# Element-wise work dealt out again between VectorE and GpSimd beside a matmul stream (attention and a split-precision FFN, one core)

## The chip, the cores and the metric

The kernel runs on one core of a Trainium2 chip. The engines are named as the profile names them: PE (TensorE's matmuls; its weight loads are PEld), DVE (VectorE), ACT (ScalarE), POOL (GpSimd) and SP (SyncE, which only issues DMAs here). The metric is the device time of one execution in microseconds (us). The kernel before took 859.63, 861.60 and 862.29 us in three runs, median 861.60.

## The reference

Local attention over 8 batches of 8 heads with 576 positions of 64 features, then a two-layer feed-forward network with an ELU on the 4608 resulting tokens, all in float32:

```python
rel = pos[:, None] - pos[None, :]
mask_plain = (rel >= 0) & (rel < 32)                     # heads 0 to 3
mask_dil = (rel >= 0) & (rel < 128) & (rel % 4 == 0)     # heads 4 to 7
scores = where(masks, q @ k.T / 8, -1e9)
attn = exp(scores - max(scores)); attn = attn / (sum(attn) + 1e-09)
x = (attn @ v) laid out as 4608 tokens x 512
h = x @ w_in                                             # 512 -> 2048
g = where(h > 0, h, exp(minimum(h, 0)) - 1)
out = g @ w_out                                          # 2048 -> 512
```

## The kernel before, in words

**Precision.** A float32 product is made of three matmuls on operands split in two: ACT casts a tile to a rounded high part (CAST in the profile), DVE subtracts it from the tile (the "rest", a TENSOR_TENSOR with an fp32r output), and PE adds high x high, high x low and low x high. A tile can be used by PE once its cast and its rest are done, in that order.

**The token axis** is cut in nine chunks of 512. Chunks 0, 1 and 2 go through the network plainly (`plain_chunk`: 16 steps f of 12 matmuls into one bank `h`, an ELU, and 12 matmuls into the output banks `o_ps`). The other six chunks are three "wide blocks" w = 0, 1, 2 of two chunks each (`wide_chunk`). There a two-by-two block product is done with seven block products in place of eight (A11, A12, S2, S1, S3, A22, S4 of the weights, against B11, B21, T2, T1, T3, T4, B22 of the tokens; S and T are sums and differences of blocks). A step of a block product is 12 matmuls of 128x128 by 128x512. "Inner" steps are the first layer, "outer" steps the second one; a block has 28 of each, and the list `wide` sets their order. An inner step's banks are added up, copied and put through the ELU by `behind_inner`, into four blocks (B11, B12, B21, B22) per group g = 0..3, tiles `a`, `a-1`, `r` of 128x1024.

**The units of the second layer.** The 28 outer steps take 28 right-hand units k in the order A11 and A12 (k = 0..7), S1 (8..11), S2 (12..15), A22 (16..19), S3 (20..23), S4 (24..27). `make_unit` makes one: `summed(k + 1)` first issues the subtraction of the next unit if it is one of the 16 of S1, S2, A22 and S3 (two blocks of 128x1024, in place), then ACT casts unit k and DVE makes its rest. A block subtracts on POOL in w = 0 and on DVE in w = 1 and 2. Units are made up to LEAD = 4 outer steps ahead in w = 0 and up to 7 in the others.

**The weight sums** S1 to S4 are made on the chip too, in jobs of "sums" steps on POOL from chunk 1 up to the first half of block 0: quarter weights loaded from memory (`whole`, `whole_out`), added, cast, their rests taken, written back (`sums_out`).

**Attention** is 32 pairs of heads and batches, laid between the network's steps. For a pair PE makes the scores (24 matmuls into two `a_ps` banks), DVE adds the masks, and `pair_steps` follows: max, less, exp, sum, more, over, times (on a tile of 96x768), six "placed" copies of 32x384 into `pt`, and "turned" (a transpose). PE then multiplies `pt` by the values `vt` (24 matmuls), and ACT copies the result to `x32`, the tokens. `pieces` lets in one set of scores or outputs at given places of PE's stream, if `scores_ready` or `output_ready` says so.

**What sets the order.** All of it is written out at build time, engine by engine, by a planner that keeps a modelled `clock` for each engine. The class `Ordered` (line 590) wraps an engine: each instruction goes through its `emit` (line 606 in the profile, whatever it does; matmuls are line 146) and moves the clock on by a fixed cost and one per element. `work(until)` (line 640) takes the step that can start first. `better` (line 632) lets POOL have a step of the kinds in SHARED (placed copies, less, times, late) as long as the phase is below SHARED_UNTIL: phase 2 is chunk two, 3 is wide block 0, 3.2 and 3.4 its later parts, 4 and 5 blocks 1 and 2. SLOWING charges a tenth of POOL's work to DVE's clock, FILL is how far past PE's clock steps are dealt out, TOLERANCE and EARLY how far past it a piece may be ready, in blocks and in chunks. On the chip each engine then runs its own list in that order and waits by semaphores for what it needs: an instruction that waits holds up all behind it on its engine.

The right-hand operands of block 0 are made by `wide_operand` at the end of chunk two and in the first five inner steps (tables at line 70): "make" is the subtraction (T1 to T4, on DVE), "cast" on ACT, "rest" on DVE. T2 and T4 start from T1 and T2.

Of the kernel before, what the change touches and what calls it, by code (L numbers as in the profile page):

```python
# [69 lines left out]
WIDE_FIRST = {"A11": "make:T1 make:T2 cast:T2 rest:T2", "A12": "cast:T1 rest:T1 make:T3", "S2": "cast:T3 rest:T3 make:T4", "S1": "cast:T4 rest:T4", "S3": "cast:B22 rest:B22"}  # L70
STORE_LAG = 1
FILL = 4.2
# [6 lines left out]
TOLERANCE = 0.3  # L79
EARLY = 0.0  # L80
# [3 lines left out]
SLOWING = 0.1  # L84
SHARED, SHARED_UNTIL = ("placed", "less", "times", "late"), 2.5
# [8 lines left out]
def body(ctx: ExitStack, tc: tile.TileContext, q, k, v, masks, w_in, w_out, out, out_t):  # L94
# [446 lines left out]
    def masks_added(hp, places, sm, eng=nc.vector):  # L541

        dil = hp >= NPAIR // 2
        for i in range(max(len(p) for p in places)):
            for h in range(2):
                n0, n1, s_ps = places[h][i]
                last = eng.tensor_tensor(out=sm[:, h * NU + n0:h * NU + n1, :].rearrange("p n j -> p (n j)"), in0=s_ps[:QB, :(n1 - n0) * 2 * G],
                                        in1=mask_sb[:, int(dil), n0 * 2 * G:n1 * 2 * G], op=ALU.add)
# [41 lines left out]
    class Ordered:  # L590
# [7 lines left out]
        def cost(self, kw):  # L598
            return self.fixed + self.each * (kw if isinstance(kw, int) else max(length(kw[n]) for n in ("out", "in_", "in0") if n in kw))

        def __getattr__(self, name):
            def emit(**kw):
                if self.name == "POOL":
                    clock["DVE"] += SLOWING * self.cost(kw)
                clock[self.name] = self.free() + self.cost(kw)
# [3 lines left out]
    vec, act, pool = Ordered(nc.vector, "DVE", 0.155, 0.00104), Ordered(nc.scalar, "ACT", 0.19, 0.00083), Ordered(nc.gpsimd, "POOL", 0.55, 0.0017)  # L609
# [16 lines left out]
    def cost(step):  # L626

        return step[1].cost(step[4] if callable(step[3]) else step[3])
# [98 lines left out]
    def pair_steps(b, hp, sm):  # L727
# [9 lines left out]
        yield ("more", b, hp), vec, "tensor_scalar", dict(out=sums, in0=sums, scalar1=1e-9, scalar2=None, op0=ALU.add)  # L737
# [59 lines left out]
    def scores_ready():  # L797
# [5 lines left out]
        if not rooms:  # L803
# [105 lines left out]
    def store(c, t, o_ps):  # L909
# [3 lines left out]
        later.append((STORE_LAG, lambda: nc.sync.dma_start(out=out[c * TC + t * P:c * TC + (t + 1) * P, :], in_=o)))  # L913
# [68 lines left out]

    def wide_operand(w, what):
# [5 lines left out]
        t = space(name in ("T2", "T4")) if name[0] == "T" else None  # L989
        j, k = {"B11": (0, 0), "B21": (1, 0), "B22": (1, 1)}.get(name, (0, 0))  # L990
        if do == "make":
            for r0, r1, (left, right) in wide_stretches(w, 0, 1):
                x0, x1 = {"T1": lambda: (right(0), left(0)), "T2": lambda: (right(1), space(0)[:, :, r0:r1]), "T3": lambda: (right(1), right(0)),
                          "T4": lambda: (left(1), space(1)[:, :, r0:r1])}[name]()
# [563 lines left out]
```

## Time and profile before

| | us |
|---|---|
| three runs, median | 859.63, 861.60, 862.29; 861.60 |
| profiled execution: its time, its span | 860.48, 858.6 |
| PE busy | 827.7 (96%) |
| DVE busy | 649.5 (76%) |
| ACT busy | 539.9 (63%) |
| POOL busy | 230.9 (27%) |
| mean granted clock | 0.988 |

The profiled execution lies 1.1 us under the median of the runs; its span, from the first to the last instruction, is 1.9 us shorter than its own time. Rows of a timeline read: start us, duration us, engine, line, operation, output <- inputs by the program's tile names, sizes, count, and in brackets the idle time before it with what ended it. Rows of the waits read: engine, what it worked on, what it waited for: total us, times, longest. Rows of windows read: start:end and length, then for each engine its busy time and its count of instructions, the granted clock as a share of full speed, the DMA share and GB/s. Chunk 0 runs up to about 80 us, chunk two ends near 355 us, block 0 near 525 us, block 1 near 690 us.

### The profile page before, as it was taken

The numbers are of one execution on the slowest core, as the hardware profiler recorded it, in microseconds if no ns is written. First come the engines' busy times: TensorE is split into PE (matmuls) and PEld (weight loads), VectorE is DVE, ScalarE is ACT, GpSimd is POOL, SyncE is SP. The second block draws the span as 40 slices with busy tenths as digits, with TensorE's granted clock in tenths as the row PEclk, the third lists the DMA queues.
The fourth block names the chain that finished last, engine by engine and source line by source line (L and its number), as shares of the span: only waits on it lengthen the run. The fifth ranks groups of instructions, "written<-read, shape, count | busy, mean of one in ns | idle before, by whom it ended". The sixth has DMA issues, their size and how long they took to land.

```text
span 858.6 us, 16052 instructions
## 1 busy us (share of the span) xinstructions
PE 827.7 (96%) x6304; PEld 653.9 (76%) x6304; DVE 649.5 (76%) x769; ACT 539.9 (63%) x912; POOL 230.9 (27%) x200
## 2 busy tenths in 40 slices
PE   6999999999999999999989789999999999999998
PEld 5566888777778778777777568878888888888886
DVE  6999996877858579868798887456769864466992
ACT  5888776765566556588777255458954545676450
POOL 3000001346376453655524980210010020000000
PEclk9999999999999999999999879999999999999999
DMA  8999879745367695799958636966656677666665
GB/s 305 372 383 366 263 232 281 213 163 163 127 220 222 170 321 187 253 399 328 293 177 244 219 97 185 327 182 185 194 175 206 205 247 220 192 189 195 200 209 169
DMA packets 105322, 199.14 MB, mean 232 GB/s; under 512 B 13120, under 2 KB 58528, under 8 KB 104992
## 3 DMA queue, kind: packets, MB, share of 16 engines
q1 hardware_dynamic: 105104, 197.81, 72.0%
q8 instruction: 50, 0.82, 0.4%
q10 hardware_dynamic: 144, 0.31, 0.1%
q14 instruction: 24, 0.20, 0.1%
HBM read 148.54 MB, written 49.55 MB: 231 GB/s over the span
## 4 chain that ended last, share of the span: by engine, by line
PE 83%; DVE 8%; ACT 5%; DMA 2%; issue 2%; DVEq 0%; SPq 0%; ACTq 0%
PE o_ps L146 43%; PE h L146 26%; PE a_ps L146 13%; DVE a L606 2%; DVE x L606 2%; DMA outputs<-a-1_3421 2%; ACT x L606 2%; DVE r L606 1%; ACT pt L533 1%; PE b L146 1%; ACT a L606 1%; DVE a-1_3421 L606 0%; DMA qt<-q 0%; DVE sm L606 0%; DVE pt L606 0%
## 5 line engine op out<-in xcount | busy, mean ns | idle before, releaser
L146 PE MATMUL o_ps<-a,r 128*128 128x512 f32 x792 | 191.6, 397 | 4.3 <-DVE a L606 3.3
L146 PEld LDWEIGHTS o_ps<-a,r 128*128 128x128 f32 x792 | 150.6, 191 | 37.6 <-DVE a L606 3.6
L146 PE MATMUL o_ps<-r,r 128*128 128x512 f32 x432 | 106.1, 397 | 4.8 <-DVE r L606 2.5
L146 PEld LDWEIGHTS o_ps<-r,r 128*128 128x128 f32 x432 | 82.2, 191 | 23.7 <-DVE r L606 3.2
L146 PE MATMUL h<-a,r 128*128 128x512 f32 x396 | 94.7, 391 | 1.1 <-ACT r L606 1.1
L146 PEld LDWEIGHTS h<-a,r 128*128 128x128 f32 x396 | 73.8, 188 | 17.3 <-ACT r L606 1.5
L146 PE MATMUL h<-x,r 128*128 128x512 f32 x324 | 80.3, 395 | 0.0
L146 PE MATMUL o_ps<-a,gh 128*128 128x512 f32 x216 | 76.2, 450 | 0.0
L146 PEld LDWEIGHTS h<-x,r 128*128 128x128 f32 x324 | 59.9, 188 | 14.6 <-DVE x L606 1.1
L606 ACT ACTIVATE x<-x 128x1024 f32<-128x1024 f32 (+1 forms) x52 | 54.3, 1046 | 13.4 <-DVE x L606 12.7
L146 PE MATMUL a_ps<-a,r 128*128 128x512 f32 x252 | 60.4, 393 | 1.2 <-DVE a L606 1.2
L606 POOL TENSOR_TENSOR a<-a 128x256 f32<-128x256 f32 (+1 forms) x57 | 52.5, 924 | 31.9 <-DMA a<-whole_out 20.3
L146 PEld LDWEIGHTS a_ps<-a,r 128*128 128x128 f32 x252 | 47.7, 190 | 12.3 <-DVE a L606 2.0
L146 PEld LDWEIGHTS o_ps<-a,gh 128*128 128x128 f32 x216 | 39.6, 188 | 17.9 <-issue 10.5
L606 POOL TENSOR_TENSOR a<-a,a 128x1024 f32<-128x1024 f32 (+2 forms) x6 | 14.9, 2488 | 128.1 <-ACT a L606 120.6
L606 DVE TENSOR_TENSOR a<-r,a 128x1024 fp32r<-128x1024 f32 x30 | 42.3, 1411 | 8.7 <-ACT a L606 8.6
L606 POOL TENSOR_TENSOR x<-x 128x256 f32<-128x256 f32 (+3 forms) x14 | 15.1, 1082 | 112.2 <-DVE a L606 98.5
L146 PE MATMUL o_ps<-r,gh 128*128 128x512 f32 x136 | 42.8, 396 | 0.0
L146 PEld LDWEIGHTS a_ps<-pt,vt 128*64 128x64 f32 x672 | 28.8, 137 | 16.8 <-issue 13.1
L606 ACT CAST a<-r 128x1024 fp32r<-128x1024 f32 x30 | 31.5, 1050 | 14.5 <-DVE r L606 12.3
L606 ACT COPY pt<-sm 32x384 f32<-32x384 f32 x65 | 33.2, 510 | 11.7 <-DVE sm L606 10.6
L146 PE MATMUL a_ps<-pt,vt 128*64 128x96 f32 x672 | 34.4, 250 | 6.3 <-issue 3.1
(229 smaller groups left out, 1647.8 us busy)
## 6 DMA issues: line engine op xcount, KB each, us to landing
r<-combined SPq DMA_DIRECT2D x84, 512.0 KB, 4.3
r<-sums_out SPq DMA_DIRECT2D x48, 512.0 KB, 4.5
r<-plain_out SPq DMA_DIRECT2D x36, 512.0 KB, 3.7
vt<-v SPq DMA_DIRECT2D x30, 384.0 KB, 4.7
kt<-k SPq DMA_DIRECT2D x29, 304.0 KB, 4.4
qt<-q SPq DMA_DIRECT2D x30, 288.0 KB, 4.0
r<-w_in SPq DMA_DIRECT2D x16, 512.0 KB, 7.1
r<-w_out SPq DMA_DIRECT2D x16, 512.0 KB, 7.4
```

The costliest lines, as they stand in the source:

```text
L146: return inorder(nc.tensor.matmul(to, w, x, **kw))
L533: inorder(nc.scalar.copy(out=to[ks, :, :, cs], in_=t4[rs, :, :, cs]))
L606: return inorder(getattr(self.eng, name)(**kw))
```

## The change

VectorE's `tensor_tensor` of the planned part is issued as `scalar_tensor_tensor` (the first input times 1.0, then the operation), except where an input lies in a PSUM bank; those go through the new `from_bank` and stay as they were. The step "more" becomes one as well. `freer` chooses DVE or POOL, whichever the planner's clocks say would end the work first, for the "make" of T1 to T4 and for the subtractions of `summed`, in all three blocks. SHARED_UNTIL goes from 2.5 to 3.5, so that POOL can get attention steps in chunk two's second half and in block 0. POOL's modelled costs change and SLOWING goes. T1 and T2 of block 0 are made in chunk two's steps 14 and 15 (in the space `a4'`), and T3, T4 and B22 each one inner step earlier. Scores are let in only while DVE's clock is at most BACKLOG = 5 us ahead of PE's; FILL, TOLERANCE and EARLY get smaller. The DMA of chunk outputs is issued one slot earlier.

```diff
                "T3": (("a0", 0, 2), ("a1", 0, 2)), "T4": (("a7", 0, 2), ("a6", 0, 2)), "B22": (("r3", 0, 1), ("r3", 2, 3))}
-WIDE_FIRST = {"A11": "make:T1 make:T2 cast:T2 rest:T2", "A12": "cast:T1 rest:T1 make:T3", "S2": "cast:T3 rest:T3 make:T4", "S1": "cast:T4 rest:T4", "S3": "cast:B22 rest:B22"}
+BEFORE = {13: "cast:B11 rest:B11", 14: "cast:B21 rest:B21 make:T1", 15: "make:T2 cast:T2 rest:T2"}
+WIDE_FIRST = {"A11": "cast:T1 rest:T1 make:T3", "A12": "cast:T3 rest:T3 make:T4", "S2": "cast:T4 rest:T4", "S1": "cast:B22 rest:B22"}
 STORE_LAG = 1
-FILL = 4.2
+FILL = 3.5
 WIDE_STEP = 4.0
...
 PIECES = {2 * G: 0.034, QB: 0.12}
-TOLERANCE = 0.3
-EARLY = 0.0
+TOLERANCE = 0.0
+EARLY = -1.0
 HOME = {2: 1, 3: 2, 4: 2.4, 5: 3.2, 6: 3.2, 7: 4.2}
...
 LEAD = 4
-SLOWING = 0.1
-SHARED, SHARED_UNTIL = ("placed", "less", "times", "late"), 2.5
+BACKLOG = 5.0
+SHARED, SHARED_UNTIL = ("placed", "less", "times", "late"), 3.5
 SUMS_FROM = 7
...
                 n0, n1, s_ps = places[h][i]
-                last = eng.tensor_tensor(out=sm[:, h * NU + n0:h * NU + n1, :].rearrange("p n j -> p (n j)"), in0=s_ps[:QB, :(n1 - n0) * 2 * G],
+                add = eng.from_bank if isinstance(eng, Ordered) else eng.tensor_tensor
+                last = add(out=sm[:, h * NU + n0:h * NU + n1, :].rearrange("p n j -> p (n j)"), in0=s_ps[:QB, :(n1 - n0) * 2 * G],
                                         in1=mask_sb[:, int(dil), n0 * 2 * G:n1 * 2 * G], op=ALU.add)
...
-        def cost(self, kw):
+        def cost(self, kw, name=None):
+            if self.name == "POOL" and name in ("copy", "tensor_copy"):
+                return 0.3 + 0.0009 * (kw if isinstance(kw, int) else length(kw["out"]))
             return self.fixed + self.each * (kw if isinstance(kw, int) else max(length(kw[n]) for n in ("out", "in_", "in0") if n in kw))
+        def from_bank(self, **kw):
+            clock[self.name] = self.free() + self.cost(kw)
+            return inorder(self.eng.tensor_tensor(**kw))
...
             def emit(**kw):
-                if self.name == "POOL":
-                    clock["DVE"] += SLOWING * self.cost(kw)
-                clock[self.name] = self.free() + self.cost(kw)
+                if self.name == "DVE" and name == "tensor_tensor":
+                    return self.scalar_tensor_tensor(out=kw["out"], in0=kw["in0"], scalar=1.0, in1=kw["in1"], op0=ALU.mult, op1=kw["op"])
+                clock[self.name] = self.free() + self.cost(kw, name)
                 return inorder(getattr(self.eng, name)(**kw))
...
-    vec, act, pool = Ordered(nc.vector, "DVE", 0.155, 0.00104), Ordered(nc.scalar, "ACT", 0.19, 0.00083), Ordered(nc.gpsimd, "POOL", 0.55, 0.0017)
+    vec, act, pool = Ordered(nc.vector, "DVE", 0.155, 0.00104), Ordered(nc.scalar, "ACT", 0.19, 0.00083), Ordered(nc.gpsimd, "POOL", 0.45, 0.00185)
+    def freer(out):
+        return min((vec, pool), key=lambda eng: eng.free() + eng.cost(length(out)))
...
-        return step[1].cost(step[4] if callable(step[3]) else step[3])
+        return step[1].cost(step[4] if callable(step[3]) else step[3], step[2])
...
         yield ("sum", b, hp), vec, "tensor_reduce", dict(out=sums, in_=sm, op=ALU.add, axis=mybir.AxisListType.X)
-        yield ("more", b, hp), vec, "tensor_scalar", dict(out=sums, in0=sums, scalar1=1e-9, scalar2=None, op0=ALU.add)
+        yield ("more", b, hp), vec, "scalar_tensor_tensor", dict(out=sums, in0=sums, scalar=1e-9, in1=sums, op0=ALU.add, op1=ALU.max)
         yield ("over", b, hp), vec, "reciprocal", dict(out=sums, in_=sums)
...
         rooms = free_sms()
-        if not rooms:
+        if not rooms or vec.free() > clock["PE"] + BACKLOG:
             return False
...
         act.copy(out=o, in_=o_ps)
-        later.append((STORE_LAG, lambda: nc.sync.dma_start(out=out[c * TC + t * P:c * TC + (t + 1) * P, :], in_=o)))
+        later.append((0, lambda: nc.sync.dma_start(out=out[c * TC + t * P:c * TC + (t + 1) * P, :], in_=o)))
...
+    def temporary(w, name):
+        if w == 0 and name in ("T1", "T2"):
+            return slots("a4'", *((0, 1) if name == "T1" else (2, 3)))
+        return space(name in ("T2", "T4"))
...
         h, l = wides[name]
-        t = space(name in ("T2", "T4")) if name[0] == "T" else None
+        t = temporary(w, name) if name[0] == "T" else None
         j, k = {"B11": (0, 0), "B21": (1, 0), "B22": (1, 1)}.get(name, (0, 0))
...
             for r0, r1, (left, right) in wide_stretches(w, 0, 1):
-                x0, x1 = {"T1": lambda: (right(0), left(0)), "T2": lambda: (right(1), space(0)[:, :, r0:r1]), "T3": lambda: (right(1), right(0)),
-                          "T4": lambda: (left(1), space(1)[:, :, r0:r1])}[name]()
-                (vec, pool)[w > 0].tensor_tensor(out=t[:, :, r0:r1], in0=x0, in1=x1, op=ALU.subtract)
+                x0, x1 = {"T1": lambda: (right(0), left(0)), "T2": lambda: (right(1), temporary(w, "T1")[:, :, r0:r1]), "T3": lambda: (right(1), right(0)),
+                          "T4": lambda: (left(1), temporary(w, "T2")[:, :, r0:r1])}[name]()
+                freer(t[:, :, r0:r1]).tensor_tensor(out=t[:, :, r0:r1], in0=x0, in1=x1, op=ALU.subtract)
         elif t is not None:
...
             for i in range(2):
-                vec.tensor_tensor(out=to[i], in0=tos[i], in1=us[key][i], op=ALU.add)
+                vec.from_bank(out=to[i], in0=tos[i], in1=us[key][i], op=ALU.add)
...
                 if to is not None:
-                    (pool if w == 0 else vec).tensor_tensor(out=to, in0=x, in1=y, op=ALU.subtract)
+                    freer(to).tensor_tensor(out=to, in0=x, in1=y, op=ALU.subtract)
...
                     cols = slice(i * TC // n, (i + 1) * TC // n)
-                    vec.tensor_tensor(out=o[:, cols], in0=tos[r][:, cols], in1=us[key][r][:, cols], op=ALU.add)
+                    vec.from_bank(out=o[:, cols], in0=tos[r][:, cols], in1=us[key][r][:, cols], op=ALU.add)
                     def write(o=o, t=t, s=s, cols=cols):
...
             finished[id(side[-1])] = clock["PE"] + LATENCY
-            if c == CS - 1 and f in (13, 14):
-                name = ("B11", "B21")[f - 13]
-                wide_operand(0, "cast:" + name)
-                wide_operand(0, "rest:" + name)
+            if c == CS - 1:
+                for what in BEFORE.get(f, "").split():
+                    wide_operand(0, what)
             pend.append((c, f, None))```

Counted over the lists of instructions: POOL has 205 rows where it had 162. Of the placed copies 39 go from ACT to POOL (POOL 11 to 50, ACT 133 to 94), of the steps less and times POOL has 11 where it had 5. Of the 16 subtractions of `summed`, block 0 keeps 9 on POOL and puts 7 on DVE (units 11, 12, 13, 14, 16, 19 and 22); in blocks 1 and 2, where DVE had all 16, POOL gets 7 of each. One attention pair whose scores lay in the last part of block 0 is let in later, in block 1. Three places follow.

POOL, last part of block 0, before, and then after. `a3`, `r1`, `r2`, `a-1` are the blocks of groups 0 to 3; the rows of 128x1024 are `summed`:

```order
L606 TENSOR_TENSOR a3_4138<-a3_4138 128x1024
L606 TENSOR_TENSOR r1_4364<-r1_4364 128x1024
L606 TENSOR_TENSOR r2_4673<-r2_4673 128x1024
L606 TENSOR_TENSOR a-1_3421<-a-1_3421 128x1024
L606 TENSOR_TENSOR a3_4138<-a4_4139,a3_4138 128x1024
L606 TENSOR_TENSOR r1_4364<-r1_4364 128x1024
L606 TENSOR_TENSOR r2_4673<-r2_4673 128x1024
L606 TENSOR_TENSOR a-1_3421<-a5_2073,a-1_3421 128x1024
```

```order
L614 TENSOR_TENSOR x1_4040<-x1_4040,nmx_4986 96x768
L614 COPY pt0_79<-x1_4040 32x12x32 x3
L614 TENSOR_TENSOR a3_4087<-a3_4087 128x1024
L614 TENSOR_TENSOR r1_4308<-r1_4308 128x1024
L614 TENSOR_TENSOR r2_4589<-r2_4589 128x1024
L614 TENSOR_TENSOR a-1_3413<-a5_2068,a-1_3413 128x1024
L614 COPY pt1_80<-sm_1487 32x12x32
L614 TENSOR_TENSOR r1_4308<-r1_4308 128x1024
```

Before, the subtractions of units 8 to 15 (S1, then S2) stand together on POOL, and those of 16 to 23 follow them. After, POOL keeps units 8, 9, 10 and 15 of these eight, then 17, with attention steps ahead of and between them.

DVE at units 12 to 14, before, and then after. Rows that write `a6` or `r3` from a block (`a3`, `r1`, `r2`) are the rests of units 12, 13 and 14; `nmx`, `sums`, `x1`, `sm` of 96 partitions are attention:

```order
L606 TENSOR_TENSOR a6_1544<-a3_4138,a7_1539 128x2x512
L606 TENSOR_REDUCE nmx_5323<-x1_4089 96x12
L606 TENSOR_TENSOR x1_4089<-x1_4089,nmx_5323 96x768
L606 TENSOR_REDUCE sums_5324<-x1_4089 96x12
L606 TENSOR_SCALAR sums_5324<-sums_5324 96x12
L606 RECIPROCAL sums_5324<-sums_5324 96x12
L606 TENSOR_TENSOR x1_4089<-x1_4089,sums_5324 96x768
L606 TENSOR_TENSOR r3_1352<-r1_4364,r3_1352 128x1024
L606 TENSOR_TENSOR sm_1487<-a_ps0_5381,masks_sb_76 96x384
L606 TENSOR_TENSOR sm_1487<-a_ps1_5382,masks_sb_76 96x384
L606 TENSOR_TENSOR r3_1352<-r2_4673,r3_1352 128x1024
```

```order
L614 SCALAR_TENSOR_TENSOR a6_1544<-a3_4087,a7_1539 128x2x512
L607 TENSOR_TENSOR sm_1487<-a_ps0_5304,masks_sb_76 96x384
L607 TENSOR_TENSOR sm_1487<-a_ps1_5305,masks_sb_76 96x384
L614 SCALAR_TENSOR_TENSOR r2_4589<-r2_4589 128x1024
L614 SCALAR_TENSOR_TENSOR r3_1352<-r1_4308,r3_1352 128x1024
L614 TENSOR_REDUCE nmx_5344<-sm_1487 96x12
L614 SCALAR_TENSOR_TENSOR sm_1487<-sm_1487,nmx_5344 96x768
L614 TENSOR_REDUCE sums_5345<-sm_1487 96x12
L614 SCALAR_TENSOR_TENSOR sums_5345<-sums_5345 96x12
L614 RECIPROCAL sums_5345<-sums_5345 96x12
L614 SCALAR_TENSOR_TENSOR sm_1487<-sm_1487,sums_5345 96x768
L614 SCALAR_TENSOR_TENSOR r3_1352<-r2_4589,r3_1352 128x1024
```

Before, the steps of one pair (from max to times) stand between the rests of units 12 and 13, and those of a second pair (whose masks are the last but one rows here) behind the rest of 14. After, the first pair stands some twenty rows earlier, the subtraction of unit 14 is on DVE, and the second pair's steps stand between the rests of 13 and 14.

POOL around the making of T3 and T4, after (`x0` is T3, `x1` T4, `a4_3926` here T1 and T2; rows of `a5` are sums jobs). Before, POOL had sums jobs alone here, and all of T1 to T4 was on DVE:

```order
L614 TENSOR_TENSOR a5_2068<-a5_2068 128x256
L614 TENSOR_TENSOR x0_4039<-x32_2762 128x2x192
L614 TENSOR_TENSOR x0_4039<-x32_2762 128x2x64
L614 TENSOR_TENSOR sm_1487<-sm_1487,sums_3847 96x768
L614 TENSOR_TENSOR a5_2068<-a5_2068 128x256 x2
L614 TENSOR_TENSOR x1_4040<-x32_1957,a4_3926 128x2x192
L614 CAST gh_4110<-a5_2068 128x512
```

So T3's first two stretches and T4's first one now stand on POOL behind sums steps; the other stretches stay on DVE.

## The prediction

> **What bounds the kernel now.** I read the page's busy shares and its chain first, then the waits of PE, then timelines of the places where PE waits. The page:
>
> ```profile
> PE   6999999999999999999989789999999999999998
> PEclk9999999999999999999999879999999999999999
> PE 83%; DVE 8%; ACT 5%; DMA 2%; issue 2%; DVEq 0%; SPq 0%; ACTq 0%
> ```
>
> PE is on the chain for 83% of the span and full but for one hole near slice 23, where the granted clock falls too. An element-wise change can only win where PE waits, or where PE runs slow after a wait. PE's waits, longest first (those of the first 80 us, which the change does not touch, left out):
>
> ```profile
> PE o_ps L146 <- DVE a L606: 3.3, 1, 3.3
> PE o_ps L146 <- DVE r L606: 2.5, 1, 2.5
> PE a_ps L146 <- DVE pt L606: 2.4, 1, 2.4
> PE o_ps L146 <- ACT r L606: 2.4, 1, 2.4
> PE a_ps L146 <- DVE a L606: 1.2, 2, 0.8
> ```
>
> These are six waits; the windows say where there are none:
>
> ```profile
> 200.00:300.00 100.00, 97.74 (x1071) 76.78 (x1069) 74.77 (x98) 59.15 (x111) 57.00 (x60) 1.00 0.61 185
> 486.00:512.00 26.00, 17.27 (x51) 12.85 (x50) 20.58 (x15) 13.93 (x21) 25.55 (x12) 0.74 0.32 104
> 512.00:600.00 88.00, 87.97 (x575) 71.33 (x575) 55.44 (x68) 52.27 (x76) 8.90 (x8) 1.00 0.70 220
> ```
>
> From 512 us on PE is full at full clock: blocks 1 and 2 have nothing to give. The 26 us from 486 are the place, with PE 66% busy, a clock of 0.74, and POOL 98% busy. PE there is at the outer steps of block 0 for units 12 to 19, and in block 1 the same stage has no wait:
>
> ```profile
> 483.30 2.99 PE L146 MATMUL o_ps<-a,r 128*128 128x512 f32 x12 [0.34 <-DMA r<-sums_out]
> 503.62 5.06 PE L146 MATMUL o_ps<-a,r 128*128 128x512 f32 x11 [3.33 <-DVE a L606]
> 519.97 5.38 PE L146 MATMUL o_ps<-r,r 128*128 128x512 f32 x23
> 647.97 11.04 PE L146 MATMUL h<-a,r 128*128 128x512 f32 x48
> 658.85 2.88 PE L146 MATMUL o_ps<-a,r 128*128 128x512 f32 x12
> 680.61 4.70 PE L146 MATMUL o_ps<-r,r 128*128 128x512 f32 x20
> ```
>
> From the first step of unit 12 to the first of unit 20 it takes 519.97 − 483.30 = 36.67 us in block 0 and 680.61 − 658.85 = 21.76 us in block 1: **14.9 us lost at one place**. Of these 8.2 are the three waits of 2.5, 2.4 and 3.3 us in the list above; most of the other 6.7 are matmuls at a lower clock behind them (11 took 5.06 us where 12 take 2.88). Why the operands were late there:
>
> ```profile
> 478.35 2.18 DVE L606 TENSOR_TENSOR x<-x,nmx 96x768 f32<-96x768 f32 x1
> 483.12 2.83 DVE L606 TENSOR_TENSOR x<-x,sums 96x768 f32<-96x768 f32 x1
> 485.99 1.55 ACT L606 COPY pt<-x 32x384 f32<-32x384 f32 x3 [4.57 <-DVE x L606]
> 488.64 2.91 DVE L606 TENSOR_TENSOR r<-r,r 128x1024 fp32r<-128x1024 f32 x1 [2.69 <-ACT r L606]
> 500.43 3.13 DVE L606 TENSOR_TENSOR a<-a-1_3421,a 128x1024 fp32r<-128x1024 f32 x1
> 482.76 5.40 POOL L606 TENSOR_TENSOR r<-r 128x1024 f32<-128x1024 f32 x2
> 444.36 0.95 DVE L606 TENSOR_TENSOR sm<-sm,nmx 96x768 f32<-96x768 f32 x1
> 644.03 1.22 DVE L606 TENSOR_TENSOR a<-a,a 128x1024 fp32r<-128x1024 f32 x1
> 428.97 2.41 POOL L606 TENSOR_TENSOR r<-r 128x1024 f32<-128x1024 f32 x1 [6.11 <-DVE a L606]
> ```
>
> The step "less" takes 0.95 us with POOL idle and 2.18 here, "times" 2.83; a rest 1.22 alone and 2.91 or 3.13 here; a POOL subtraction 2.41 alone and 2.7 here. DVE and POOL hold each other up, one instruction at a time. And an attention pair stands ahead of units 13 and 15: unit 13's cast stands on ACT behind three copies that waited 4.57 us for "times".
>
> **The change part by part.** The sum goes against the profiled execution, 860.48 us, and 1.1 us are added at the end, since the three runs' median is 861.6.
>
> *A, subtractions and attention in the last part of block 0.* DVE takes 7 of the 16 subtractions, 7 × 1.22 = 8.5 us more for it and 7 × 2.7 = 19 us less for POOL. One pair stands some twenty rows earlier, and one leaves the block: max, less, sum, times and two small steps, with the waits for ACT between them, no longer stand ahead of unit 13's rest, nor copies ahead of its cast. That takes away the 2.4 and 2.5 us waits and the slow matmuls behind them. The second pair stays, now between the rests of units 13 and 14, with POOL's subtractions 15, 17 and 18 beside it; so part of what now shows as 3.33 us before unit 15 can come up at unit 14. I leave a third of the loss: **−10**; ends −14.9 (all of it) and −3 (the waits of unit 13 gone and a new one of 2.5 us at unit 14, with matmuls behind it at half the pace).
>
> *B, T1 to T4.* PE's two waits of 1.2 us in the list are for the rests of T3 and T4:
>
> ```profile
> 358.89 2.79 PE L146 MATMUL a_ps<-a,r 128*128 128x512 f32 x11 [0.79 <-DVE a L606]
> 357.45 1.38 DVE L606 TENSOR_TENSOR a<-x,a 128x1024 fp32r<-128x1024 f32 x1 [1.11 <-ACT a L606]
> 381.04 3.18 POOL L606 TENSOR_TENSOR a<-a 128x256 f32<-128x256 f32 x4 [4.29 <-DMA a<-whole_out]
> ```
>
> Both are made one inner step earlier, 2.7 us of PE or more, against 0.79 and 0.39 of wait. Against it, two stretches of T3 and one of T4 now stand on POOL behind sums steps, which can wait for a DMA as in the last row (4.29 us). The moved steps issue no DMA of their own. **−1**; ends −1.2 and +2 (such a wait, less the step gained).
>
> *C, the output piece at 443 us.* Its wait was for "turned", late by a "times" that met a POOL step, and PE paid twice:
>
> ```profile
> 443.64 1.21 PE L146 MATMUL a_ps<-pt,vt 128*64 128x96 f32 x24 [2.38 <-DVE pt L606]
> 444.78 4.60 PE L146 MATMUL o_ps<-a,r 128*128 128x512 f32 x12
> 435.59 3.15 DVE L606 TENSOR_TENSOR x<-x,sums 96x768 f32<-96x768 f32 x1
> 434.68 3.25 POOL L606 TENSOR_TENSOR r<-r 128x1024 f32<-128x1024 f32 x1 [3.29 <-DVE r L606]
> ```
>
> That is 2.38 + (4.60 − 2.88) = 4.1 us. TOLERANCE 0 and BACKLOG let pieces in later, which makes such a wait less likely: **−2**; ends −4.1 and 0. Pieces let in later cost nothing as long as pairs are left over: one pair goes from block 0 to block 1, where DVE is busy 55.44 of 88 us.
>
> The clock after this wait bears on A too. The Trainium skill, "TensorE: Matmul & The Clock Gate", section "Part 1: The HAM clock gate", says that the clock halves only after an idle window of about 3.4 us; by it waits of 2.4 us would cost themselves alone, A could bring 8.2 at most, and the forecast would be some 4 us higher, 855. The rows differ: twelve matmuls took 4.60 us a little behind an idle of 2.38, so I keep the price with the slow matmuls; 855 lies within the forecast's own range.
>
> *D, more steps on POOL.* From the groups of instructions:
>
> ```profile
> L606 POOL COPY pt<-sm 32x384 f32<-32x384 f32 x7 | 4.4, 631 | 17.6 <-PE a_ps L146 16.5 <-DVE sm L606 1.0
> L606 ACT COPY pt<-sm 32x384 f32<-32x384 f32 x65 | 33.2, 510 | 11.7 <-DVE sm L606 10.6
> L606 POOL TENSOR_TENSOR sm<-sm,nmx 96x768 f32<-96x768 f32 x2 | 3.3, 1662 | 3.3 <-DVE nmx L606 3.3
> ```
>
> 39 copies are 39 × 0.63 = 25 us more for POOL and 39 × 0.51 = 20 us less for ACT; 6 steps of 96x768 are 6 × 1.66 = 10 us more for POOL and 6 × 0.95 = 6 less for DVE. None is waited for by PE directly: "turned" waits for the copies, and an output piece for it. But each such step on POOL can hold up a DVE step by its length, and those of DVE between a unit's cast and PE have little slack. If one in ten of the 45 made a wait like that at 443 us it would be 4.5 × 4.1 = 18 us; but in the window from 200 us, with POOL at 57%, PE was idle for no more than 2.3 us of 100. I take **+3**, under one such wait; ends 0 and +12 (three of them).
>
> *E, the form.* With `scalar_tensor_tensor` nothing is gained or lost by itself. The trace has the ELU's, on two SBUF operands:
>
> ```profile
> 372.78 1.56 DVE L606 SCALAR_TENSOR_TENSOR a<-a,x 128x1024 f32<-128x1024 f32 x1
> 376.91 1.22 DVE L606 SCALAR_TENSOR_TENSOR a<-a,x 128x1024 f32<-128x1024 f32 x1
> 388.62 1.29 DVE L606 SCALAR_TENSOR_TENSOR r<-r,x 128x1024 f32<-128x1024 f32 x1
> 388.78 4.19 POOL L606 TENSOR_TENSOR x<-x 128x256 f32<-128x256 f32 x4
> ```
>
> 1.22 us, as the plain form has (644.03 above); and beside POOL one takes 1.56, and the four POOL steps at 388.78 take 4.19 us where four of this form took 3.18 at 381.04. So it and POOL still wait for each other: **0**. But no long POOL step lies ahead of one of these rows, so that it waits less than the plain form is not excluded; this makes the third rival.
>
> *F, blocks 1 and 2.* POOL takes 7 of 16 subtractions, 2.41 us in place of 1.22. There units are made up to 7 ahead; the rest at 644.03, of unit 8, ends at 645.25, and PE begins units 8 to 11 with the 48 matmuls at 647.97. A collision of 1.9 us, as in the rest at 500.43, fits in these 2.7: **0**; ends 0 and +3 (one such wait and slow matmuls behind it). The earlier issue of chunk stores on SP, "more" in another form, and POOL's modelled cost alone: 0, since PE waits for none of them in the list.
>
> Sum: −10 − 1 − 2 + 3 + 0 = −10, 850.5 us against 860.48; with 1.1, **851 us**.
>
> **Rivals.** *R1, slower.* POOL's new steps in chunk two and block 0 hold DVE up, "turned" comes late, and output pieces wait, each for 4.1 us as at 443 us. It decides where D passes the 13 us of A, B and C, from a fourth such wait on; with four, A at −10, and B and C at nothing, it is 861.6 − 10 + 4 × 4.1 = 868. For it: PE's waits at 443 and 488 are both of this kind, and POOL's rows grow from 162 to 205. Against it: BACKLOG holds scores back when DVE is behind, and ACT loses 20 us. The Trainium skill, "Perfetto Trace Analysis", section "Optimizing Scalar/DVE Operations", warns that GpSimd and DVE share a port and that moving work between the two may not help; the trace agrees, by rests of 2.91 us beside 1.22.
>
> *R2, the hole only moves.* Unit 14's rest stands behind a whole pair, as unit 13's did; PE waits there for what it waited for before, and A brings 3 of 14.9, B and C nothing: 861.6 − 3 = 859. For it: the pair between the rests of 13 and 14. Against it: the unit is made up to four steps ahead, and a step is 21.76 / 8 = 2.72 us; and POOL has fewer subtractions there.
>
> *R3, the change does more than its rows show.* `scalar_tensor_tensor` does not wait for a running POOL step; the rests stay at 1.22 us, and A, B and C all come at their ends with D at nothing: 861.6 − 14.9 − 1.2 − 4.1 = 841, less some 2 us of smaller waits: about 839. For it: 1.29 us at 388.62. Against it: 1.56 at 372.78.
>
> **How the numbers follow.** My forecast has 0.58 (843 to 858 by itself), R1 0.17, R2 0.15, R3 0.10. About 0.3%, 2.6 us, is what a measurement of this kernel can tell from no change, so faster is below 859.0. Faster: 0.57 of the forecast, half of R2, all of R3, which is 0.74; same: 0.01 of the forecast, most of R2's other half and a little of R1, 0.10; slower: the rest of R1 and of R2, 0.16. The range from 839 to 865 leaves out half of R3, some two thirds of R1 and a trace of the forecast, 0.18.
>
> **What would show it.** A: from unit 12's first matmul to unit 20's some 27 us in block 0, a clock above 0.9 there, no wait for a rest of `r` over 1 us. B: no wait of `a_ps` for DVE's `a` near 359 us. C and D: in chunk two and block 0, waits for `pt` add up to under 5 us. E: rests on DVE beside POOL's steps still between 1.3 and 3 us. F: from the start of block 1 on PE as full as now. The forecast is wrong if a hole as long as the one removed stands at another unit or at output pieces (R1, R2), or if rests stay at 1.22 beside a running POOL step (R3).

## The result, and the profile after

The changed kernel takes **866.0 us** (median of four executions from 864.79 to 866.64; the kernel before, measured beside it, 861.2), a ratio of **1.0056** with an interval of 1.0036 to 1.0075: slower, where 851 was forecast. The profiled execution took 864.79 us against 860.48, 4.3 us more. All numbers here are of undisturbed executions; of one experiment (the subtractions on POOL in the kernel before) there is no such profile, and only its times and its lists of instructions are used.

On the page of the changed kernel the hole near slice 23 is shallower (8 tenths busy in slices 22 and 23, with the clock at 9 or more), and there are two new ones, at slices 31 and 38:

```profile
PE   6999999999999999899998899999996999999798
PEclk9999999999999999999999999999998999999999
PE 76%; DVE 12%; DMA 5%; ACT 4%; issue 2%; SPq 0%; DVEq 0%; POOL 0%; ACTq 0%
```

DMA's share of the chain went from 2 to 5%, DVE's from 8 to 12. PE's waits have a new first row (four of the rows):

```profile
PE o_ps L147 <- DMA r<-sums_out: 11.8, 2, 6.8
PE o_ps L147 <- DVE a L614: 4.6, 2, 3.3
PE o_ps L147 <- ACT r L614: 1.5, 1, 1.5
PE o_ps L147 <- DVE r L614: 1.3, 2, 1.0
```

Of the three waits at units 12 to 20 of block 0 (2.4, 2.5, 3.3 us) one of 3.3 is left, and the wait for `pt` is gone. Some ten us behind its place, though, from 451 to 458 us, there are three waits that were not there (1.3, 1.5 and 1.0 us), and 11 matmuls behind them take 4.26 us. Two waits for a DMA, also new, are larger than all that went. PE's timeline, from unit 12 to unit 20 of blocks 0, 1 and 2:

```profile
478.33 2.88 PE L147 MATMUL o_ps<-a,r 128*128 128x512 f32 x12
490.14 2.79 PE L147 MATMUL o_ps<-a,r 128*128 128x512 f32 x11 [3.27 <-DVE a L614]
506.06 5.60 PE L147 MATMUL o_ps<-r,r 128*128 128x512 f32 x24
646.22 3.19 PE L147 MATMUL o_ps<-a,r 128*128 128x512 f32 x12
659.52 4.45 PE L147 MATMUL o_ps<-r,r 128*128 128x512 f32 x12 [6.78 <-DMA r<-sums_out]
677.40 5.60 PE L147 MATMUL o_ps<-r,r 128*128 128x512 f32 x24
807.98 2.88 PE L147 MATMUL o_ps<-a,r 128*128 128x512 f32 x12
818.95 4.91 PE L147 MATMUL o_ps<-r,r 128*128 128x512 f32 x12 [5.00 <-DMA r<-sums_out]
837.31 5.60 PE L147 MATMUL o_ps<-r,r 128*128 128x512 f32 x24
```

Block 2 of the kernel before, for comparison (blocks 0 and 1 are shown above):

```profile
811.17 2.88 PE L146 MATMUL o_ps<-a,r 128*128 128x512 f32 x12
832.93 5.60 PE L146 MATMUL o_ps<-r,r 128*128 128x512 f32 x24
```

| unit 12 to unit 20 | before, us | after, us | difference |
|---|---|---|---|
| block 0 | 36.67 | 506.06 − 478.33 = 27.73 | −8.9 |
| block 1 | 21.76 | 677.40 − 646.22 = 31.18 | +9.4 |
| block 2 | 832.93 − 811.17 = 21.76 | 837.31 − 807.98 = 29.33 | +7.6 |

The gain in block 0 came about as forecast, and blocks 1 and 2, where PE was full before, lost 17.0 us. The rest, 4.3 − 8.1 = −3.8 us, is for the most part ahead of unit 12 of block 0, which starts 5.0 us earlier (478.33 in place of 483.30; 1.0 of this is the set of scores that is let in later); between unit 20 of block 0 and unit 12 of block 1, 1.3 us are lost again.

Why the weights come late: DVE, POOL and SP's queue ahead of the wait in block 1.

```profile
628.52 3.44 DVE L614 SCALAR_TENSOR_TENSOR r<-a,r 128x1024 fp32r<-128x1024 f32 x1
643.12 3.43 DVE L614 SCALAR_TENSOR_TENSOR a<-a,a 128x1024 fp32r<-128x1024 f32 x1
646.47 6.48 DVE L614 SCALAR_TENSOR_TENSOR r<-r,r 128x1024 fp32r<-128x1024 f32 x2
652.87 1.27 DVE L607 TENSOR_TENSOR gh<-o_ps,hh 128x512 f32<-128x512 f32 x2
642.07 3.39 POOL L614 TENSOR_TENSOR a-1_3413<-a,a-1_3413 128x1024 f32<-128x1024 f32 x1
630.09 11.20 SPq L964 DMA_DIRECT2D r<-sums_out  x5
653.58 0.94 SPq L1195 DMA_DIRECT2D out_t<-gh  x2
654.61 0.91 SPq L964 DMA_DIRECT2D r<-sums_out  x2
```

Read it from the bottom. The load that PE waits for until 659.52 was issued at 654.61. Ahead of it on SP's queue stand two stores of C11 (`gh`), which could go only when DVE had made their additions, from 652.87 on. DVE was late because six of its instructions there took some 3.4 us in place of 1.2, each beside one on POOL, whose subtractions took 3.4 in place of 2.4. In the whole kernel SP waited five times for `gh` from DVE, 23.1 us in sum (before three times, 5.7 us):

```profile
SPq L1195 <- DVE gh L607: 23.1, 5, 12.3
```

Why the stores are ahead, the order of SP's queue tells. Before the change all eight loads of units 8 to 15 went out first:

```profile
640.01 19.36 SPq L952 DMA_DIRECT2D r<-sums_out  x8
659.50 0.34 SPq L1177 DMA_DIRECT2D out_t<-gh  x1
```

In the changed kernel the stores stand ahead of the loads of units 14 and 15 (below). The program keeps DVE's instructions in its own order, but leaves SP's to the scheduler, which it asks to go by a simulated timeline (line 1568 of the changed kernel). We take it that in this simulation DVE, with seven instructions fewer, ends sooner, and so the stores move up; experiment 1 shows that they fall back when the seven return.

```order
L964 DMA r0_932<-sums_out1_113 128x1024
L1195 DMA out_t<-gh_6604 128x512
L1195 DMA out_t<-gh_6606 128x512
L964 DMA r0_932<-sums_out2_114 128x1024
L964 DMA r0_932<-sums_out3_115 128x1024
```

### The profile page after: what moved, and what is told of

It reads as the page before. It is cut to its first block, busy times and chain, and to the rows that moved or that the text cites. A ratio compares the mean times of both kernels' runs of the same rounds, so it can differ in the third digit from the quotient of the medians.

```text
span 863.0 us, 16083 instructions
## 1 busy us (share of the span) xinstructions
PE 825.8 (96%) x6304; PEld 651.5 (75%) x6304; DVE 650.9 (75%) x758; ACT 519.7 (60%) x873; POOL 286.9 (33%) x250
## 2 busy tenths in 40 slices
PE   6999999999999999899998899999996999999798
## 4 chain that ended last, share of the span: by engine, by line
PE 76%; DVE 12%; DMA 5%; ACT 4%; issue 2%; SPq 0%; DVEq 0%; POOL 0%; ACTq 0%
PE o_ps L147 39%; PE h L147 24%; PE a_ps L147 13%; DVE a L614 5%; DVE r L614 4%; ACT x L614 1%; DMA outputs<-a-1_3413 1%; DMA r<-sums_out 1%; DMA r<-combined 1%; DMA r<-w_in 1%; DMA vt<-v 1%; ACT a L614 1%; DVE a-1_3413 L607 0%; DMA qt<-q 0%; DVE a-1_3413 L614 0%
## 5 line engine op out<-in xcount | busy, mean ns | idle before, releaser
L147 PE MATMUL o_ps<-a,r 128*128 128x512 f32 x792 | 188.7, 392 | 4.6 <-DVE a L614 4.6
L147 PEld LDWEIGHTS o_ps<-a,r 128*128 128x128 f32 x792 | 147.5, 188 | 37.6 <-DVE a L614 5.8
L147 PE MATMUL o_ps<-r,r 128*128 128x512 f32 x432 | 109.7, 405 | 15.7 <-DMA r<-sums_out 11.8
L147 PEld LDWEIGHTS o_ps<-r,r 128*128 128x128 f32 x432 | 84.0, 196 | 36.6 <-issue 12.6
L614 POOL TENSOR_TENSOR a<-a 128x256 f32<-128x256 f32 (+1 forms) x59 | 59.3, 1009 | 126.0 <-DVE r L614 116.6
L147 PE MATMUL h<-a,r 128*128 128x512 f32 x396 | 94.3, 390 | 0.0
L147 PEld LDWEIGHTS h<-a,r 128*128 128x128 f32 x396 | 74.0, 188 | 15.9
L147 PE MATMUL h<-x,r 128*128 128x512 f32 x324 | 79.7, 395 | 0.0
L147 PE MATMUL o_ps<-a,gh 128*128 128x512 f32 x216 | 76.1, 449 | 0.0
L147 PEld LDWEIGHTS h<-x,r 128*128 128x128 f32 x324 | 60.1, 188 | 13.8 <-DVE a L188 0.2
L147 PE MATMUL a_ps<-a,r 128*128 128x512 f32 x252 | 60.2, 391 | 3.0 <-DVE a L614 1.5
L614 ACT ACTIVATE x<-x 128x1024 f32<-128x1024 f32 (+1 forms) x53 | 54.9, 1041 | 8.3 <-POOL x L614 7.6
L147 PEld LDWEIGHTS a_ps<-a,r 128*128 128x128 f32 x252 | 46.9, 188 | 14.7 <-DVE a L614 2.8
L614 DVE SCALAR_TENSOR_TENSOR a<-a,a 128x1024 fp32r<-128x1024 f32 (+2 forms) x32 | 47.6, 1492 | 7.7 <-ACT a L614 7.3
L614 DVE SCALAR_TENSOR_TENSOR a<-r,a 128x1024 fp32r<-128x1024 f32 x30 | 45.7, 1530 | 10.0 <-ACT a L614 10.0
L147 PEld LDWEIGHTS o_ps<-a,gh 128*128 128x128 f32 x216 | 39.7, 188 | 17.8 <-issue 10.5
L614 ACT CAST a<-r 128x1024 fp32r<-128x1024 f32 x30 | 31.3, 1047 | 34.5 <-DVE r L614 27.1
L614 POOL TENSOR_TENSOR sm<-sm,nmx 96x768 f32<-96x768 f32 x4 | 5.9, 1472 | 126.4 <-DMA out<-e 121.1
L614 ACT CAST a<-a 128x1024 fp32r<-128x1024 f32 (+1 forms) x30 | 28.9, 962 | 29.6 <-DVE a L614 18.3
L147 PE MATMUL o_ps<-r,gh 128*128 128x512 f32 x136 | 42.7, 395 | 0.0
L614 ACT COPY e<-o_ps 128x512 f32<-128x512 f32 x44 | 24.8, 587 | 28.2 <-PE o_ps L147 24.8
L614 DVE SCALAR_TENSOR_TENSOR gl<-e,gh 128x512 fp32r<-128x512 f32 x34 | 28.1, 827 | 17.7 <-ACT gh L614 14.0
```

Source lines behind the costliest of these rows:

```text
L147: return inorder(nc.tensor.matmul(to, w, x, **kw))
L614: return inorder(getattr(self.eng, name)(**kw))
```

## The experiments

**Theory T**: POOL's subtractions in blocks 1 and 2 hold DVE up, so the additions of C11 are late; their stores hold SP's queue up, so weights are late. **Rivals**: U, the loads are late for attention moved into block 1; V, the new form of DVE's instructions does it. The changed kernel and the first three experiments make a square: subtractions on POOL or on DVE, stores ahead of the two loads or behind.

**1. Blocks 1 and 2 back on DVE** (the stores fall back behind the loads by themselves).

```diff
-                    freer(to).tensor_tensor(out=to, in0=x, in1=y, op=ALU.subtract)
+                    (freer(to) if w == 0 else vec).tensor_tensor(out=to, in0=x, in1=y, op=ALU.subtract)
```

> The changed kernel with the 16 subtractions of blocks 1 and 2 back on DVE (POOL loses 14 instructions; the order by which SP is served follows: the stores of C11 stand behind the loads for units 14 and 15 again). Theory T: in the changed kernel POOL's seven subtractions per block hold the rests on DVE up (3.4 us for 1.2), the additions of C11 come late, their stores block SP's queue, the weight loads behind them come late (waits of 6.8 and 5.0 us, then a slow clock). T expects both waits for sums_out gone and 866.0 - 17 = 849 us. Rival U: the loads come late because attention or its transfers moved into block 1: then 866 and the waits stay. Rival V: the new form of DVE's instructions does it: 866.

Measured: 848.0 us, ratio to the kernel before 0.9858 (0.9838 to 0.9879). Both waits for `sums_out` are gone. DVE in block 1:

```profile
627.55 1.22 DVE L614 SCALAR_TENSOR_TENSOR r<-a,r 128x1024 fp32r<-128x1024 f32 x1
644.57 1.29 DVE L607 TENSOR_TENSOR gh<-o_ps,hh 128x512 f32<-128x512 f32 x2
```

From the rest that writes `r<-a,r` to the additions DVE ran 15 instructions in 644.57 − 627.55 = 17.0 us. In the changed kernel it ran 10 there in 652.87 − 628.52 = 24.4. With fewer instructions it needed 7.3 us more. PE's and ACT's lists of instructions are the same in both kernels, attention included: only 14 subtractions change engine and, in each block, the two stores change place. T holds. U falls, since attention was not moved back, and V, since the new form stayed.

**2. Only the two stores put behind the loads**, subtractions left on POOL.

```diff
-            nc.sync.dma_start(out=to, in_=src)
+            last_load[:] = [nc.sync.dma_start(out=to, in_=src).ins]
...
+                        def behind(write=write):
+                            with tc.issue_after(last_load[0]):
+                                write()
-                        later.append((STORE_LAG, write))
+                        later.append((4, behind) if name == "C11" and w else (STORE_LAG, write))
```

> The changed kernel with nothing moved but SP's queue in blocks 1 and 2: the two stores of C11 stand behind the loads for units 14 and 15, as they did in the kernel before; POOL keeps its seven subtractions. T in its strong form (the late additions cost only through the store ahead of the loads): no wait for sums_out, rests on DVE still 3.4 us, 850 to 853 us. If the late rests stall PE by themselves: waits for DVE's r or a of 2 us or more in both blocks and 856 to 862. U: 866.

The two stores are also written four steps later in place of one; in the lists nothing but the place of these rows on SP's queue differs from the changed kernel.

Measured: 849.8 us, ratio 0.9875 (0.9856 to 0.9893). DVE's rests are as slow as in the changed kernel, but PE has no wait for `sums_out`, and at units 12 to 14 of block 1 only one wait for a rest, of 0.3 us:

```profile
641.15 3.43 DVE L614 SCALAR_TENSOR_TENSOR a<-a,a 128x1024 fp32r<-128x1024 f32 x1
628.14 16.64 SPq L964 DMA_DIRECT2D r<-sums_out  x7
651.59 0.94 SPq L1195 DMA_DIRECT2D out_t<-gh  x2
```

In this stretch seven loads go out ahead of the stores, where five did. So the price of some 16 us hangs on two rows of SP's queue.

**3. Only the two stores held ahead**, subtractions on DVE as in experiment 1.

```diff
+            with tc.issue_after(stored_first[0]) if stored_first else ExitStack():
+                last_load[:] = [nc.sync.dma_start(out=to, in_=src).ins]
...
+                            with tc.issue_after(last_load[0]):
+                                stored_first[:] = [write()]
+                        later.append((2, ahead) if name == "C11" and w else (STORE_LAG, write))
```

> The kernel with the subtractions of blocks 1 and 2 on DVE, but the two stores of C11 held two loads ahead on SP's queue, as in the changed kernel. T: the additions end some 0.7 us behind the time at which the load for unit 15 went out before, so the load for unit 14 is about 3 us late and has as much slack: 849 to 852, a wait for sums_out under 1 us. A rival, the place in the queue alone: the waits of 5 to 7 us stay, 866.

Measured: 849.8 us, ratio 0.9877 (0.9860 to 0.9894). The waits for `sums_out` are small:

```profile
PE o_ps L147 <- DMA r<-sums_out: 1.5, 2, 0.9
```

The place in the queue alone costs next to nothing either (two waits of 0.9 us or less). Against experiment 1, late additions alone cost 1.9 us and stores ahead alone 1.8, neither clear of the intervals; both together cost 18: the slack of a load covers either, not both.

**4. The kernel before, with seven subtractions of blocks 1 and 2 on POOL.**

```diff
-                    (pool if w == 0 else vec).tensor_tensor(out=to, in0=x, in1=y, op=ALU.subtract)
+                    (pool if w == 0 or k in (8, 9, 11, 12, 14, 15, 16) else vec).tensor_tensor(out=to, in0=x, in1=y, op=ALU.subtract)
```

> The kernel before with one thing done: the seven subtractions (units 8, 9, 11, 12, 14, 15, 16) of blocks 1 and 2 on POOL, with DVE's plain form. SP's queue follows, the stores of C11 two loads earlier. T: both waits for sums_out appear, 861.2 + 17 = 878 us. U and V: 861, no such wait.

Measured: 878.9 us, ratio 1.0216 (1.0190 to 1.0243), with DVE's plain form and attention where it was. The loss can be had from this one part alone. The lists show nothing else moved but the two stores of each block, which stand ahead of the loads of units 14 and 15 here too; that PE waits there as in the changed kernel was not seen.

The next four start from experiment 1 (848.0 us) and take single terms of the prediction.

**5. All 16 subtractions of block 0 on POOL again.** Edit: `pool if w == 0 else vec`.

> The kernel with blocks 1 and 2 on DVE (848.0 us) and all 16 subtractions of block 0 back on POOL; attention's place unchanged. If the dealing out of block 0's subtractions is what took the hole of units 12 to 20 from 36.7 to 27.8 us, it comes back: 848 + 9 = 857. If it was the attention pair that was moved away from there: 848, with a hole of 26 to 30 us.

Measured: 854.3 us, ratio 0.9927 (0.9902 to 0.9952). Unit 12 starts at 479.96 and unit 20 at 509.61 us, 29.7 us:

```profile
479.96 2.96 PE L147 MATMUL o_ps<-a,r 128*128 128x512 f32 x12
490.31 4.21 PE L147 MATMUL o_ps<-r,r 128*128 128x512 f32 x11 [2.31 <-DVE r L614]
509.61 0.39 PE L147 MATMUL o_ps<-r,r 128*128 128x512 f32 x1
```

In between both expectations. With all 16 on POOL, as before the change, this stage takes 29.7 us where it took 36.7: 7.0 of the 8.9 us come from the rest of the change (the attention pairs that stand elsewhere are the likely part, not tried alone), and 1.9 from dealing the subtractions out. In the profiled executions the two kernels differ by 7.3 us: 2.8 are there before unit 12, 1.9 in this stage and 2.5 behind it. Where the 2.8 arise, in chunk two and early in block 0, both kernels have the same instructions in the same order, so they are a difference between executions and not what the edit did.

**6. DVE's instructions in the plain form.**

```diff
-                if self.name == "DVE" and name == "tensor_tensor":
+                if False:
...
-        yield ("more", b, hp), vec, "scalar_tensor_tensor", dict(out=sums, in0=sums, scalar=1e-9, in1=sums, op0=ALU.add, op1=ALU.max)
+        yield ("more", b, hp), vec, "tensor_scalar", dict(out=sums, in0=sums, scalar1=1e-9, scalar2=None, op0=ALU.add)
```

> The kernel with blocks 1 and 2 on DVE, and nothing else than DVE's instructions put back into the plain form (tensor_tensor, tensor_scalar); the order of every engine is the same. Term E of the prediction (the form itself is worth nothing): 848 within 2 us, rests beside POOL's subtractions 2.5 to 3.4 us in both. Third rival of the prediction (the form waits less for POOL): 853 or more.

Measured: 848.2 us, ratio 0.9860 (0.9841 to 0.9879); experiment 1 had 0.9858. Beside the same subtraction on POOL the rest of unit 15 takes the same time in the plain form (first row) and in the new one (second row, of experiment 1):

```profile
487.07 3.37 DVE L614 TENSOR_TENSOR a<-a-1_3413,a 128x1024 fp32r<-128x1024 f32 x1
```

```profile
485.61 3.36 DVE L614 SCALAR_TENSOR_TENSOR a<-a-1_3413,a 128x1024 fp32r<-128x1024 f32 x1
```

The form is worth nothing that can be measured.

**7. All subtractions on DVE, in block 0 too.** Edit: `vec` in place of `freer(to) if w == 0 else vec`.

> The kernel with blocks 1 and 2 on DVE, and all 16 subtractions of block 0 on DVE too. T (a subtraction given to POOL costs DVE more than it spares it): DVE's rests in block 0 back at 1.2 us, the wait of 3.3 us at unit 15 and the slow matmuls behind it gone, 842 to 845. Its rival (block 0 has attention besides, and DVE cannot do all): waits for DVE's rests of units 12 to 23 grow, 850 to 856.

Measured: **842.8 us**, ratio **0.9808** (0.9782 to 0.9835), the fastest of all (the rows are of its slowest execution, 846.06 us). Unit 12 to unit 20 take 501.52 − 478.62 = 22.9 us, of which 0.9 is a set of scores that the planner now lets in between them:

```profile
478.62 2.88 PE L147 MATMUL o_ps<-a,r 128*128 128x512 f32 x12
490.64 11.04 PE L147 MATMUL a_ps<-a,r 128*128 128x512 f32 x48
501.52 5.60 PE L147 MATMUL o_ps<-r,r 128*128 128x512 f32 x24
```

With 16, 9 and 0 subtractions of block 0 on POOL the medians are 854.3, 848.0 and 842.8 us: some 0.7 us for each.

**8. The right-hand operands of block 0 as before.** Edit: the old tables, and `(vec, pool)[w > 0]` for the "make" of T1 to T4.

> The kernel with blocks 1 and 2 on DVE, and the right-hand operands T1 to T4 and B22 of block 0 made where and by whom they were before (all on DVE, T1 and T2 in block 0). The planner deals some attention out again behind it. Term B of the prediction: 848 + 1 = 849, the two waits for T3 and T4 (0.8 and 0.4 us) back near 350 us. If it is worth more (DVE's load at the start of block 0): 852 or more.

Measured: 848.8 us, ratio 0.9858 (0.9826 to 0.9889). Nothing that can be measured. Of the two waits one came back, of 0.44 us. In the changed kernel PE waits at the same place for weights instead:

```profile
355.71 3.02 PE L147 MATMUL o_ps<-r,r 128*128 128x512 f32 x12 [1.07 <-DMA r<-combined]
360.25 2.96 PE L147 MATMUL a_ps<-a,r 128*128 128x512 f32 x12 [1.51 <-DMA r<-combined]
```

The last ones ask what of the change is left beside the subtractions.

**9. The kernel before with all subtractions on DVE**, one line and nothing else of the change (the planner then deals some of attention out again).

```diff
-                    (pool if w == 0 else vec).tensor_tensor(out=to, in0=x, in1=y, op=ALU.subtract)
+                    vec.tensor_tensor(out=to, in0=x, in1=y, op=ALU.subtract)
```

> The kernel before with one thing done: the 16 subtractions of block 0 on DVE, as blocks 1 and 2 have them; nothing else of the change. If the 16 subtractions are the hole of block 0 by themselves: its 14.9 us go, 860 - 15 = 845. If the two attention pairs that stand at units 12 to 15 are its cause, and the change's later letting in is needed as well: a hole of 25 to 36 us stays and 852 to 860.

> The kernel before with the 16 subtractions of block 0 on DVE once more, for its profile: from unit 12 to unit 20 of block 0 it took 36.7 us before and 27.8 us with the changed kernel's dealing out. If DVE's share of the subtractions is what counts: 22 to 24 us, rests at 1.2 us, some 848 us in all. If the attention pairs at units 12 to 15 are: 28 us or more, and the gain of some 12 us lies elsewhere.

Measured: 847.9 and 847.1 us, ratios 0.9867 (0.9835 to 0.9900) and 0.9841 (0.9805 to 0.9876). The stage takes 502.89 − 480.99 = 21.9 us, and the window in which POOL was busy for 25.55 of 26 us before has PE full:

```profile
486.00:512.00 26.00, 26.00 (x117) 21.52 (x116) 25.94 (x24) 15.06 (x20) 13.63 (x3) 1.00 0.63 202
480.12 1.22 DVE L606 TENSOR_TENSOR r<-r,r 128x1024 fp32r<-128x1024 f32 x1 [0.71 <-ACT r L606]
490.14 0.95 DVE L606 TENSOR_TENSOR x<-x,sums 96x768 f32<-96x768 f32 x1
```

With the 16 subtractions off POOL the hole of the kernel before is gone. Attention's steps stand among the rests here too (of one pair the sum to the times, of the second its masks and max); with POOL out of the way less and times take 0.95 us each, and no unit is late. The planner has put the second pair's less, sum and times behind this stage, and what that alone is worth was not tried. By experiment 5 other places for attention take away 7.0 us of the hole with all 16 still on POOL, so the hole came of the two standing together. Against experiment 7 (842.8) the rest of the change is worth some 4 us, which the intervals do not separate from nothing.

**10. Pieces let in as before** (FILL 4.2, TOLERANCE 0.3, EARLY 0, no BACKLOG), from experiment 7.

> The kernel with all subtractions on DVE (842.8 us) and FILL, TOLERANCE, EARLY and BACKLOG as before the change: pieces let in earlier, the rest as changed. Term C of the prediction (pieces let in later take waits for pt away): 842.8 + 2 = 845, a wait for pt of 2 us or more. If the rules for letting in are worth nothing: 843 within 2. If the attention pairs' place made the gain of block 0: 850 or more.

Measured: 857.6 us, ratio 0.9968 (0.9959 to 0.9977). The number lies in the third expectation, its reason does not: the loss of 15 us is not for `pt`, and for the most part not in block 0, but in chunk two, where two waits are new:

```profile
PE a_ps L147 <- ACT a-1_3436 L614: 3.6, 1, 3.6
PE o_ps L147 <- ACT gh L614: 3.4, 1, 3.4
308.89 0.80 ACT L614 COPY a-1_3436<-a_ps 128x288 f32<-128x288 f32 x2 [6.71 <-DMA outputs<-a-1_3436]
```

In the first, ACT's copy of an output piece waits 6.71 us for a store to leave its tile (third row), and PE behind it for the bank; in the second the ELU of a chunk step is late. Together they are 7.0 us; slower matmuls behind them add to it, and the rest was not split up. The kernel before has the same values without such waits, and experiment 9, which keeps them, is at 847. So these values cost that much only together with what else the change put into chunk two. What of that it is was not tried.

**11. The 20 placed copies that POOL has from the middle of chunk two on, issued on ACT**, from experiment 7.

```diff
+        if eng is pool and name[0] == "placed" and phase[0] >= 2.5:
+            clock["POOL"] = pool.free() + pool.cost(kw, op)
+            ins = inorder(nc.scalar.copy(**kw))
```

> The kernel with all subtractions on DVE (842.8 us), and the 20 placed copies that POOL has from the middle of chunk two on issued on ACT instead, every other instruction in the same order. Term D of the prediction (POOL's new steps hold DVE up): 842.8 - 3 = 840. If the copies on POOL spare ACT more than they cost DVE: 845 or more. If neither: 843 within 2.

Measured: 846.2 us, ratio 0.9835 (0.9811 to 0.9859) where experiment 7 had 0.9808 (0.9782 to 0.9835). Slower by 3 us in the medians, but the intervals overlap, and the two profiled executions differ by 1.4 us: unclear. On SP's queue, which follows by itself, the stores of the weight sums also change places with loads beside them, so the copies are not the only thing that moved. ACT's cast of an ELU is late in chunk two:

```profile
343.87 0.78 PE L147 MATMUL o_ps<-r,gh 128*128 128x512 f32 x2 [2.35 <-ACT gh L614]
```

## Why the prediction was wrong

**F, blocks 1 and 2, is the step that failed.** It stood at 0, with ends 0 and +3, and measured +17.0 us (9.4 and 7.6). What it said of the rests themselves held: by experiment 2 late rests alone cost PE some 2 us at most. But it stopped at PE's wait for a rest. It priced one collision of 1.9 us; six in a row made DVE 7.3 us late for what stands behind the rests, the additions of C11. DVE could not make this up: in the kernel before it was busy for all of the 19 us from 640 to 659 and from 793 to 812 us, while the prediction had read its share between 512 and 600 us (55.44 of 88). And of SP's queue it looked at the chunk stores alone, and put them at nothing. The order of that queue, which is fixed when the kernel is built, has two stores moved up by two loads; behind the late additions these made the loads late, in waits of 6.78 and 5.00 us with slow matmuls behind them.

**A was right**: −8.9 us measured, −10 forecast, 27.7 us for the stage where "some 27" was named, a clock of 1.00 from 486 to 512 us. By experiment 5 most of it, 7.0 us, is not the dealing out of the subtractions. The wait left is at unit 15, for the rest of the changed block `a-1`, not at unit 14. Its cause was half seen: the price of POOL beside DVE was read from the rows, but the sum counted the seven moved subtractions as 8.5 us more for DVE. By experiments 5, 7 and 9 the stage gets shorter with each step that puts more of them on DVE, down to 21.9 us from 36.67 when all 16 stand there (experiment 9).

**B** was nothing that can be measured (experiment 8), which −1 does not contradict: the waits for T3 and T4 went, and 1.07 and 1.51 us of waits for weights came at their place. **C**: the wait for `pt` went, but the three waits from 451 to 458 us came behind its place, and the rules for letting in weigh more than the 2 us given to them, in the other parts' company (experiment 10). **D**: the 3 us that copies on POOL were to cost did not show; without them the kernel got no faster, and if anything slower (experiment 11, unclear). The attention steps on POOL (less, times) were not tried alone. **E** was right: 0 (experiment 6), and the third rival, which hung on it, fell.

The sum itself is 850.48 + 1.1 = 851.6, which was rounded down. **R1**, slower at 868, is nearest to the time, but that is luck: it has the right collision in the wrong place, not "turned" and output pieces in chunk two and block 0, but stores and loads in blocks 1 and 2. **R2** did not come. Of what would show the forecast wrong, "F: PE as full as now" from block 1 on was the line that did.

The Trainium skill, "SBUF — State Buffer", section "Who interferes with whom", says that the pair of ports which DVE and GpSimd share is an exclusive lock, and that a DVE instruction with two inputs in SBUF contends with a GpSimd instruction that reads SBUF. The rows agree, for both forms (3.43 and 3.37 us): 3.43 us on DVE is its own 1.22 and 2.2 of POOL's. Followed through, a subtraction given to POOL spares a busy DVE 1.22 us and takes 2.2 from it.

## What to carry to other kernels

Before a share of one engine's work goes to its neighbour, price what the neighbour's instruction takes from the first engine where both are busy: here 2.2 us for 1.22 spared, and the 16 subtractions of block 0 were best all on the engine that seemed the fuller one. Where an engine gets later or earlier in a planner's model, read what moves on the queues behind it, DMA queues first: here a store that waited held two loads behind it. A stage with no wait at all has no gain to give, but it can lose; count its slack over a whole run of instructions, not for one, and up to the last engine or queue that waits for them.

## What the runs showed of the hardware

A slow clock behind a wait is not a fixed price. The two profiles of the changed kernel and of experiment 1 have the same wait at the same place, 3.27 and 3.32 us; behind the one, 11 matmuls took 2.79 us (granted clock 1.00 from 490 to 493 us), behind the other 4.23 (0.64 from 489 to 493.3 us):

```profile
489.02 4.23 PE L147 MATMUL o_ps<-a,r 128*128 128x512 f32 x11 [3.32 <-DVE a L614]
```

In the kernel before, a wait of 2.38 us and a piece of 1.21 were followed by 12 matmuls in 4.60 (0.59 from 445 to 449 us). So here waits of 2.4 to 3.3 us cost themselves alone once, and 1.4 to 1.7 us more twice. The prediction's sums took the dearer price each time, so they were no more exact than this.
